# Attention beside an FFN: four fixed stages for each FFN block in an attention step

## The chip, the cores and the metric

One core of a Trainium2 chip runs the whole program. The metric is the device time of one execution in microseconds (us), the median of several runs. The core has TensorE (PE in the profile, with PEld for its weight loads), VectorE (DVE), ScalarE (ACT), GpSimd (POOL) and SyncE (SP), which here issues nearly all DMAs. Each works through its own queue in order; engines wait for each other through semaphores.

## The reference

Attention in which a query sees only the keys of its own hash bucket, and then a feed-forward network (FFN) on its result:

```python
q_bits = (np.einsum('bhsd,dk->bhsk', q, proj) > 0)      # 6 bits; k the same
mask = q_bucket[:, :, :, None] == k_bucket[:, :, None, :]
scores = np.where(mask, scale * q @ k.T, -1e9)
attn = softmax(scores)                                   # over the keys
x = (attn @ v) as [batch * seq, heads * head_dim]
h = x @ w_in
out = (h * np.clip(h + 3.0, 0.0, 6.0) / 6.0) @ w_out
```

There are 4 batches, 8 heads, 768 positions, head size 64, so 32 heads in all; x is 3072 x 512, w_in 512 x 2048, w_out 2048 x 512. All is float32. The kernel keeps that precision with products of split numbers: each operand is a rounded part (high) plus the rest (low), and high x high, high x low and low x high are summed.

## The kernel before

**Attention** goes by steps. A step handles 128 queries of one head against its 768 keys, so a head is six steps and there are NS = 192. In step k the loop does, for different rows g of the pipeline:

- `scores(k + 3)`, inside `lead` (L909): four PE matmuls into the tile s. Outside the beginning there is a single such tile (`pair`, L102, tag "s", one buffer); the hash matmuls z of the next head use the same one.
- `lowest(k + 2)` (L355): DVE reads s, writes p and its row minimum m, which frees s.
- `exponential(k + 1)` (L366): ACT, in place on p.
- `flip(k + 1)` and `move(k)` (L390, L398): from step GT on, p is turned without PE. DVE transposes 32 x 32 blocks into f, SP writes f to DRAM (fd), and four DMAs bring it back turned, into one of two tiles (`spare` for even rows, `px` for odd ones).
- `split_p` (L415): ACT casts the turned row into the high part ph, and DVE (first half of the keys) or POOL (second half) subtracts to the low part pl. Before GT the row is turned by PE transposes (pt) instead. The subtractions are collected in `lows` and issued by `split_lows` (L444).
- `value_half` and `values` (L452): at every second step, twelve PE matmuls, ph and pl of two rows times the split values vv, into acc. `output` (L470) copies acc to y on ACT, SP stores it to the DRAM tile xs, and `add` (L465) lets a POOL DMA add the other half to it.

`lead` also prepares the next head, by t = (k + 3) mod 6: at t = 0 `split_qk` (L268; ACT copy qq, three SP DMAs, POOL subtractions kk and qq), at t = 2 `split_v` (POOL) and the loads, at t = 4 `scale_q` (L261). `hash_qk` and `bits` follow at t = 2 as well.

**The FFN** goes by chunks of 256 positions, twelve in all, and by 16 blocks `fc` in each chunk. A block is `gemm1` (L562, twelve matmuls into h), `gate` (L585: ACT relu into g, DVE product with h, ACT cast into gb's first half gh, POOL or, in the last batch, DVE subtraction into gb's second half gl), and `gemm2` (L597, six wide matmuls into po), which is issued one block later. g and gb have one buffer each in this part of the program. The three chunks of batch 0 run by themselves early on. The other nine come from the generator `ffn` (L817): whatever calls `next(fill)` gets its next piece. Between chunks a list `side` holds the work that loads, normalises and splits the next chunk's inputs.

**Order.** PE, DVE, ACT and POOL stand in the order of the code (`manual_schedule`); the DMAs on SP are put in order by a scheduler when the program is built. GF = 2 * 48 + FS and GT = GF + FT set where the loop changes: `next(fill)` is first called at step GF - 2 = 102, and from step GT - 1 = 105 each step is a call of `beside_ffn` (L971). This function calls `next(fill)` twice: after `split_p` (gemm1 of a block), and after the hash (gemm2 of the block before, then the gate). What is left of the FFN when attention has ended runs alone.

Of the kernel before, what the change touches and what calls it, by code (L numbers as in the profile page):

```python
# [10 lines left out]
F32 = mybir.dt.float32  # L11
# [16 lines left out]

LA = 3
FB = 4  # L30
FS = 8
FT = 2
LT = 2
WL = 30
# [9 lines left out]
def lsh_attention_moe(  # L44
# [31 lines left out]
    def dma(out: bass.AP, in_: bass.AP):  # L76
        nonlocal last
        last = nc.sync.dma_start(out=out, in_=in_)

    ob_turn = 0  # L80
    spare = []

# [172 lines left out]
    def spans(i: int):  # L255


        n = 4 if i <= 2 else 2 if i > GF // KT + 1 else 1
        return [slice(x * S // n, (x + 1) * S // n) for x in range(n)]

    def scale_q(i: int):  # L261

        for c in spans(i):
            nc.gpsimd.tensor_scalar_mul(raws[i][:D, c], raws[i][:D, c], -SCALE)

    copied = None

# [176 lines left out]
    def split_lows():  # L444
        for f in lows:
            f()
        lows.clear()
# [135 lines left out]
        return x[:, 0], x[:, 1]  # L583

    def gate(n: str, fc: int, hp, copy, engine, between=lambda: None):  # L585
        g = sp.tile([P, TC], F32, name=f"g{n}_{fc}", tag="g", bufs=1)
        gh, gl = gate_tiles(f"{n}_{fc}")
        nc.scalar.activation(g[:], hp[:], AF.Relu, bias=three[:], scale=1.0)  # L588
        nc.vector.scalar_tensor_tensor(  # L589
            out=g[:], in0=g[:], scalar=6.0, in1=hp[:], op0=ALU.min, op1=ALU.mult  # L590
        )
        between()
        copy(gh, g[:])  # L593
        engine.tensor_sub(gl, g[:], gh.bitcast(F32))  # L594
        return gh, gl

    def gemm2(fc: int, po, gh, gl):  # L597
        wo = wt[2 * fc + 1]
# [27 lines left out]
    def beside():  # L626
        if side:
            side.pop(0)()
# [105 lines left out]
    def first_ffn(resume):  # L734
        nonlocal ffn_on
        ffn_on = True
        normalise("late0", lt(0), late["rb"][0], "pt")
        split_x(x0[0][cc3], lt(0), nc.vector)
        room12(0)
        for c in range(cc3):  # L740
            split_x(x0[1][c], xr0[1][:, c], (nc.vector, nc.gpsimd)[c % 2])
        normalise("late1", lt(1), late["rb"][1], "pt")
        yield

        room12(1)
# [12 lines left out]
        def finish(fc: int, t: int, gg):  # L758
            gemm2(fc, pos[t], *gg)
            return (lambda: store(0, t, pos[t])) if fc + 1 == NFC else None  # L760


        begun = WA
        stage = {WA - 1: 2}
        for n, (fc, t) in enumerate(order):
            if n == 1:
                pos[2] = [bank([P, DM], f"pt0_{u}", "pt")[:] for u in range(2)]
            hp = gemm1(f"0_{t}", fc, x0[t], "pu")
            new = None
            if begun < NW and n and n % 4 != 3 and n >= ready.get(begun, 0):  # L770
                new = begun
                begun += 1
            at = dict(stage)

            for x in [x for x in at if at[x] == 5]:
                cv(x)

            def between():

                if new is not None:  # L780
                    cv(new)
                for x in [x for x in at if at[x] == 3]:
                    cv(x)

            gg = gate(f"0_{t}", fc, hp, nc.scalar.copy, nc.vector, between)
# [24 lines left out]
            if n >= len(order) - 3:  # L810
                resume(n - len(order) + 3)
        yield
        finish(*pend)()
        ffn_on = False
        yield

    def ffn():  # L817
        nonlocal ffn_on
# [8 lines left out]
        def begin(c: int):  # L827
# [3 lines left out]
            xr[c] = load_x(b, t, range(NCC))  # L831
            todo = scale_x(b, t, range(NCC), xr[c])
            if b < B - 1:
                side.extend([lambda: None] * 2 + todo)
                return

            side.extend([lambda: None] * (4 if t else 6) + todo[:2])
# [28 lines left out]
        for c, (b, t) in enumerate(chunks):  # L866
            while not there(c):
                if pend is not None:
                    finish()()
                yield  # L870
            n = f"{b}_{t}"
            if c not in xr:
                begin(c)
            while side:
                beside()
                yield
                yield
            if c not in xhl:
                place(c)
                for cc in range(NCC):  # L880
# [3 lines left out]
            po = None  # L884
            for fc in range(NFC):
                hp = gemm1(n, fc, xhl[c])
                yield
                end = finish() if pend is not None else lambda: None
                if po is None:
                    po = ps.tile([P, 2, 512], F32, name=f"po{n}", tag="s" if b == B - 1 and t % 2 == 0 else "po", bufs=1)  # L890
                gg = gate(n, fc, hp, copy, engine)
                end()
                pend = ((b, t), (fc, [po[:, u] for u in range(2)], *gg))
                if c + 1 < len(chunks) and c + 1 not in xr and there(c + 1):
                    if fc >= XF[chunks[c + 1][0] == B - 1]:
                        begin(c + 1)
                if fc + 1 == NFC and c + 1 in xr and c + 1 not in xhl and not side:
                    place(c + 1)
                    for cc in range(NCC):
                        split(c + 1, cc)  # L900
                else:
                    beside()
                yield
                beside()
            del xhl[c]
        finish()()

# [1 line left out]
    def lead(j: int):  # L909
# [3 lines left out]
        alone = j < GF + LA  # L913
        if t == 0 and n < NJ:
            split_qk(n, nc.scalar.copy if ffn_on else nc.gpsimd.tensor_copy)
        if t in (1, 4):
            add()
        if t == 2:
            if i:
# [41 lines left out]
    with tc.manual_schedule(engines={ET.PE, ET.DVE, ET.Activation, ET.Pool}):  # L961
# [6 lines left out]
            ahead(0, x)  # L968
        for _ in range(2):
            cv(0)  # L970
        def beside_ffn(k: int):  # L971

            for c in range(2):
                if k < GT:
                    transp(k, c)
            whole = False
            for _ in range(1 if k < GT else 2):
                u = vnext // 2
                if u < NS // 2 and (k < GT or k % 2 == 0 and k >= 2 * u + 2 + (LT if 2 * u >= GT else 0)):
                    whole = value_half()  # L980
            if k + 1 < NS:
                exponential(k + 1)
            late = k if k < GT else k - LT
            if GT <= late < NS or k < GT:
                for c in range(2):
                    split_p(late, c, False)
            next(fill, None)
            if whole:
                output(vnext // 2 - 1)
            if k == NS + LT - 1:  # L990
# [12 lines left out]
            if k + LA < NS:  # L1003
                lead(k + LA)
            else:
                add()

        for k in range(NS + LT):
            if k >= GT - 1:
                beside_ffn(k)  # L1010
                continue
# [59 lines left out]
            if k + 1 == GB:  # L1071
# [3 lines left out]
                    whole = value_half()  # L1075
                output(vnext // 2 - 1)
                next(first)
        while vnext < NS:
            if value_half():
                output(vnext // 2 - 1)  # L1080
        add()
        for _ in fill:
            pass
# [47 lines left out]
```

## Time and profile before

| | us |
|---|---|
| median of 3 runs | 1090.09 (1090.05 to 1092.1) |
| the profiled execution | 1093.36 |
| its span in the trace | 1091.3 |

Busy time in that span: PE 994.0 us (91%), PE weight loads 894.3, DVE 707.4, ACT 623.6, POOL 567.9. A busy PE is not a PE at its peak, since the profile models the ends of matmuls and a matmul at half clock is busy twice as long. So shares of the whole say little here. The profile is read by stages: attention alone and with the first FFN chunks (to about 406 us), attention beside the FFN (to about 894 us), and the FFN alone. The starts of L360 (`lowest`, once a step) mark the steps: row 105 at 406.29 us, row 112 at 437.40, row 191 at 893.68. The granted clock of PE is 1.0 at full speed and 0.5 when it is halved.

### The profile page before, as it was taken

To read this page: it belongs to the slowest core of one execution; us is meant where nothing else is said; L and a number is where in the kernel's file an instruction comes from. 1 tells how busy PE (TensorE), PEld (TensorE's weight loads), DVE (VectorE), ACT (ScalarE), POOL (GpSimd) and SP (SyncE) were. 2 spreads that over 40 slices of the span, in tenths; PEclk is the share of its full clock that TensorE was granted. 3 is DMA by queue.
4 is the path that set the end of the run, shared out by engine and by line. 5 is a ranking of instruction groups with operands and counts; after the bars stand their busy time and mean duration, and the time that the engine had idled before them with its cause. 6 is when DMAs were issued, how large, how long until landed. Compare 5 with 4: busy or idle time off the path is not lost.

```text
span 1091.3 us, 19386 instructions
## 1 busy us (share of the span) xinstructions
PE 994.0 (91%) x6330; PEld 894.3 (82%) x6330; DVE 707.4 (65%) x1350; ACT 623.6 (57%) x1407; POOL 567.9 (52%) x662
## 2 busy tenths in 40 slices
PE   8999999999999996888888878878877999999998
PEld 7999888888899995778777768767776978899897
DVE  6999988897699996566556655656655662233332
ACT  5888865555788884455454545454445554333332
POOL 6777625565377765566556645664666453301000
PEclk8999999999999997999899999998989999999999
DMA  3566585000355556675666666675657653001000
GB/s 108 152 150 163 150 305 205 1 1 6 106 120 119 120 132 187 196 212 174 198 199 171 186 187 196 182 209 169 197 158 223 179 167 91 20 20 40 1 20 20
DMA packets 109340, 148.37 MB, mean 136 GB/s; under 512 B 12804, under 2 KB 78724, under 8 KB 109240
## 3 DMA queue, kind: packets, MB, share of 16 engines
q1 hardware_dynamic: 104760, 141.64, 42.8%
q0 software_dynamic: 4480, 5.51, 4.3%
q8 instruction: 50, 0.82, 0.3%
q14 instruction: 50, 0.41, 0.1%
HBM read 75.76 MB, written 51.90 MB: 117 GB/s over the span
## 4 chain that ended last, share of the span: by engine, by line
PE 56%; DVE 12%; DMA 9%; issue 7%; POOL 7%; ACT 6%; SPq 2%; DVEq 0%; POOLq 0%; ACTq 0%
PE pt L382 5%; PE h L569 5%; PE acc L460 5%; PE h L570 5%; PE h L568 5%; PE po L601 5%; PE po L603 5%; PE po L602 4%; PE acc L461 4%; PE s L351 4%; DMA spare<-fd 4%; PE s L353 4%; DVE pl L440 3%; DVE p L360 2%; POOL qq L298 2%
## 5 line engine op out<-in xcount | busy, mean ns | idle before, releaser
L360 DVE TENSOR_SCALAR_CACHE_REDUCE p<-s 128x768 f32<-128x768 f32 x192 | 183.5, 956 | 26.9 <-PE pt L382 13.8
L372 ACT ACTIVATE p<-p,m 128x768 f32<-128x768 f32 x192 | 179.8, 936 | 18.3 <-DVE p L360 17.7
L593 ACT CAST gb<-g 128x256 fp32r<-128x256 f32 x137 | 55.7, 407 | 213.5 <-DVE g L589 136.2
L393 DVE STREAM_TRANSPOSE f<-p 128x768 f32<-128x768 f32 x86 | 84.0, 977 | 126.3 <-ACT p L372 85.0
L588 ACT ACTIVATE g<-h,three 128x256 f32<-128x256 f32 x192 | 91.0, 474 | 128.3 <-PE h L570 112.1
L594 POOL TENSOR_TENSOR gb<-g,gb 128x256 fp32r<-128x256 f32 x89 | 65.5, 736 | 172.0 <-ACT gb L593 170.1
L460 PE MATMUL acc<-ph,vv 128*128 128x256 f32 x564 | 151.0, 299 | 2.5 <-DVE pl L440 2.4
L589 DVE SCALAR_TENSOR_TENSOR g<-g,h 128x256 f32<-128x256 f32 x192 | 80.0, 417 | 108.6 <-ACT g L588 108.0
L568 PE MATMUL h<-xh,w 128*128 128x256 f32 x512 | 146.4, 286 | 0.7 <-ACT xh L559 0.7
L461 PE MATMUL acc<-pl,vv 128*128 128x256 f32 x564 | 142.9, 286 | 4.3 <-DVE pl L440 4.3
L569 PE MATMUL h<-xl,w 128*128 128x256 f32 x512 | 145.6, 284 | 0.2 <-DVE xl L560 0.2
L570 PE MATMUL h<-xh,w 128*128 128x256 f32 x512 | 144.7, 283 | 0.0
L351 PE MATMUL s<-kk,qq 76*128 76x384 f32 x384 | 108.1, 363 | 27.3 <-DVE p L360 25.3
L461 PEld LDWEIGHTS acc<-pl,vv 128*128 128x128 f32 x564 | 109.1, 193 | 5.3 <-DVE pl L440 5.2
L460 PEld LDWEIGHTS acc<-ph,vv 128*128 128x128 f32 x564 | 108.9, 193 | 5.4 <-PE pt L382 2.0
L439 ACT CAST ph<-pt 128x384 fp32r<-128x384 f32 x204 | 91.4, 473 | 26.7 <-PE pt L382 15.8
L440 DVE TENSOR_TENSOR pl<-pt,ph 128x384 fp32r<-128x384 f32 x204 | 104.0, 550 | 2.5 <-ACT ph L439 1.9
L353 PE MATMUL s<-kk,qq 128*128 128x384 f32 x384 | 103.3, 351 | 0.0
L351 PEld LDWEIGHTS s<-kk,qq 76*128 76x128 f32 x384 | 65.2, 197 | 46.4 <-DVE p L360 28.0
L601 PE MATMUL po<-w,gb 128*128 128x512 f32 x242 | 100.3, 414 | 3.0 <-ACT ob L617 2.0
L569 PEld LDWEIGHTS h<-xl,w 128*128 128x128 f32 x512 | 97.9, 191 | 3.1 <-DVE xl L560 0.6
L568 PEld LDWEIGHTS h<-xh,w 128*128 128x128 f32 x512 | 97.8, 191 | 2.6 <-ACT xh L559 1.0
(163 smaller groups left out, 2552.4 us busy)
## 6 DMA issues: line engine op xcount, KB each, us to landing
fd<-f SPq DMA_DIRECT2D x86, 384.0 KB, 3.5
spare<-fd SPq DMA_DIRECT2D x172, 96.0 KB, 2.6
px<-fd SPq DMA_DIRECT2D x172, 96.0 KB, 2.7
raw<-in_qkT SPq DMA_DIRECT2D x32, 384.0 KB, 3.3
kk<-qq SPq DMA_DIRECT2D x62, 192.0 KB, 3.2
wr<-in_w_in SPq DMA_DIRECT2D x16, 512.0 KB, 10.8
wr<-in_w_out SPq DMA_DIRECT2D x16, 512.0 KB, 3.9
vr<-in_v SPq DMA_DIRECT2D x32, 192.0 KB, 2.6
```

The costliest lines, as they stand in the source:

```text
L351: nc.tensor.matmul(s[:, c, :HW], lhsT=q1[:KM, us], rhs=half(k1[:KM], c), start=True, stop=False)
L353: nc.tensor.matmul(s[:, c, :HW], lhsT=q2[:, us], rhs=half(k2, c), start=False, stop=True)
L360: nc.vector.tensor_scalar(out=pr_[:], in0=s[:, :, :HW], scalar1=CAP, scalar2=None, op0=ALU.min, op1=ALU.min, accum_out=m[:],)
L372: nc.scalar.activation(pr_[:], pr_[:], AF.Exp, bias=m[:], scale=-1.0, accum_out=sms[b][:, t, h : h + 1])
L439: nc.scalar.copy(hi, pt)
L440: lows.append(lambda: engine.tensor_sub(lo, pt, hi.bitcast(F32)))
L460: nc.tensor.matmul(acc[:], lhsT=vv[:, kt], rhs=hi[:, x], start=(kt == 0), stop=False)
L461: nc.tensor.matmul(acc[:], lhsT=vv[:, kt], rhs=lo[:, x], start=False, stop=(kt == KT - 1))
L568: nc.tensor.matmul(hp[:], lhsT=wi[:, 0, wc], rhs=xh, start=(cc == 0), stop=False)
L569: nc.tensor.matmul(hp[:], lhsT=wi[:, 0, wc], rhs=xl, start=False, stop=False)
L570: nc.tensor.matmul(hp[:], lhsT=wi[:, 1, wc], rhs=xh, start=False, stop=(cc == NCC - 1))
L601: nc.tensor.matmul(po[u], lhsT=gh[:, us], rhs=wo[:, 0], start=(fc == 0), stop=False)
```

## The change

Each block of the FFN beside attention is cut into four stages, A to D, and `beside_ffn` has one place for each. `go("A")` runs the generator only if that is the stage it stands at.

- A, after the exponential: the split of the gate (gh on ACT, gl on POOL) of the block begun in the step before. `gate` now returns a function that does it.
- B, after the casts `split_p`: gemm1. (The pieces before the first block run here too, one a step.)
- C, after minimum, outputs and hash: gemm2 of the block before, and relu and product of this block.
- D, at the end of the step: the work of `side`.

Other edits in the same function: `split_lows` (pl on DVE and POOL) stands behind stage C and `lead` instead of ahead of them; `output` runs in the step after its values; `add` runs at k mod 6 = 2 and 4, behind D, instead of in `lead`. `scale_q` runs on ACT once `paced` is set, and `spans` no longer cuts the later heads in two. FS goes from 8 to 10, so the first call of the generator is at step 104 and `beside_ffn` starts at step 107. The loop runs two steps longer, without attention rows. When it ends, blocks go on unstaged as before.

```diff
-FS = 8
+FS = 10
@@ spans, scale_q
-        n = 4 if i <= 2 else 2 if i > GF // KT + 1 else 1
+        n = 4 if i <= 2 else 1
...
+            if paced:
+                nc.scalar.mul(raws[i][:D, c], raws[i][:D, c], -SCALE)
+            else:
+                nc.gpsimd.tensor_scalar_mul(raws[i][:D, c], raws[i][:D, c], -SCALE)
@@ gate
         between()
-        copy(gh, g[:])
-        engine.tensor_sub(gl, g[:], gh.bitcast(F32))
-        return gh, gl
+        def split():
+            gh, gl = gate_tiles(f"{n}_{fc}")
+            copy(gh, g[:])
+            engine.tensor_sub(gl, g[:], gh.bitcast(F32))
+            return gh, gl
+        return split
@@ ffn
                 hp = gemm1(n, fc, xhl[c])
+                stage = "C"
                 yield
                 end = finish() if pend is not None else lambda: None
...
+                parted = paced
+                split_g = gate(n, fc, hp, copy, engine)
+                if not parted:
+                    gg = split_g()
                 end()
...
+                if parted:
+                    stage = "D"
+                    yield
+                    for _ in range(-(-len(side) // (NFC - fc))):
+                        beside()
                 if fc + 1 == NFC and c + 1 in xr and c + 1 not in xhl and not side:
                     place(c + 1)
                     for cc in range(NCC):
                         split(c + 1, cc)
-                else:
+                elif not parted:
                     beside()
+                if parted:
+                    stage = "A"
+                    yield
+                    gg = split_g()
+                pend = ((b, t), (fc, [po[:, u] for u in range(2)], *gg))
+                stage = "B"
                 yield
-                beside()
+                if not parted:
+                    beside()
@@ lead
-        if t in (1, 4):
+        if t in (1, 4) and not paced:
             add()
@@ beside_ffn
                 if u < NS // 2 and (k < GT or k % 2 == 0 and k >= 2 * u + 2 + (LT if 2 * u >= GT else 0)):
-                    whole = value_half()
+                    if value_half():
+                        through.append(vnext // 2 - 1)
             if k + 1 < NS:
                 exponential(k + 1)
+            go("A")
             late = k if k < GT else k - LT
             if GT <= late < NS or k < GT:
                 for c in range(2):
                     split_p(late, c, False)
-            next(fill, None)
-            if whole:
-                output(vnext // 2 - 1)
+            go("B")
...
             if k + 2 < NS:
                 lowest(k + 2)
+            paced = True
+            while through and (through[0] < vnext // 2 - 1 or k % 2 or k < GT):
+                output(through.pop(0))
+            if k + LA < NS and (k + LA) % KT == 2 and (k + LA) // KT + 1 < NJ:
+                hash_qk((k + LA) // KT + 1)
+                bits((k + LA) // KT + 1)
+            go("C")
+            if k + LA < NS:
+                lead(k + LA)
             split_lows()
             if GT <= k < NS:
                 move(k)
-            if k + LA < NS and (k + LA) % KT == 2 and (k + LA) // KT + 1 < NJ:
-                hash_qk((k + LA) // KT + 1)
-                bits((k + LA) // KT + 1)
-            next(fill, None)
-            if k + LA < NS:
-                lead(k + LA)
-            else:
+            go("D")
+            if k % KT in (2, 4):
                 add()
-        for k in range(NS + LT):
+        for k in range(NS + LT + 2):
```

Where this puts instructions is shown at one place of the program, steps 147 and 148, where head 26 is split. In the names, kk_26 and qq_26 are that head's low parts, pl72 and ph72 the parts of rows 144 (from `spare`) and 145 (from `px`), with _0 or _1 for the half of the keys, and gb1_2_4 is the gate of batch 1, chunk 2, block 4.

POOL before:

```order
L264 TENSOR_SCALAR raw26_7959<-raw26_7959 64x384 x2
L440 TENSOR_TENSOR pl72_1_8100<-spare_5537,ph72_1_8099 128x3x128
L594 TENSOR_TENSOR gb1_2_4_8139<-g1_2_4_8138,gb1_2_4_8139 128x256
L440 TENSOR_TENSOR pl72_1_8100<-px_5704,ph72_1_8099 128x3x128
L594 TENSOR_TENSOR gb1_2_5_8185<-g1_2_5_8184,gb1_2_5_8185 128x256
L296 TENSOR_TENSOR kk_26_8190<-raw26_7959,qq_26_8191 64x384 x2
L298 TENSOR_TENSOR qq_26_8191<-raw26_7959,qq_26_8191 64x384 x2
L440 TENSOR_TENSOR pl73_1_8223<-spare_5537,ph73_1_8222 128x3x128
```

POOL of the changed kernel at the same place (its lines are numbered a little higher):

```order
L602 TENSOR_TENSOR gb1_2_1_8019<-g1_2_1_7990,gb1_2_1_8019 128x256
L445 TENSOR_TENSOR pl72_1_8026<-spare_5610,ph72_1_8025 128x3x128
L602 TENSOR_TENSOR gb1_2_2_8069<-g1_2_2_8054,gb1_2_2_8069 128x256
L301 TENSOR_TENSOR kk_26_8107<-raw26_7862,qq_26_8108 64x768
L303 TENSOR_TENSOR qq_26_8108<-raw26_7862,qq_26_8108 64x768
L445 TENSOR_TENSOR pl72_1_8026<-px_5780,ph72_1_8025 128x3x128
L602 TENSOR_TENSOR gb1_2_3_8140<-g1_2_3_8104,gb1_2_3_8140 128x256
L445 TENSOR_TENSOR pl73_1_8147<-spare_5610,ph73_1_8146 128x3x128
```

The scale (raw26) is gone from POOL. The low part of row 145, pl72_1 from px, stood ahead of kk_26 and qq_26 and now stands behind them. On PE the matmuls acc72, which read pl72_1, stand in both kernels right behind the scores of row 150, the last work of step 147.

ACT before, from the exponential of step 147 on:

```order
L372 ACTIVATE p148_8124,sms3_7905<-p148_8124,m148_8123 128x768
L439 CAST ph72_0_8096<-px_5704 128x3x128
L439 CAST ph72_1_8099<-px_5704 128x3x128
L588 ACTIVATE g1_2_5_8184<-h1_2_5_8152,three_68 128x256
L593 CAST gb1_2_5_8185<-g1_2_5_8184 128x256
L290 CAST qq_26_8191<-raw26_7959 128x768
L372 ACTIVATE p149_8170,sms3_7905<-p149_8170,m149_8169 128x768
```

ACT of the changed kernel:

```order
L377 ACTIVATE p148_8046,sms3_7811<-p148_8046,m148_8045 128x768
L601 CAST gb1_2_2_8069<-g1_2_2_8054 128x256
L444 CAST ph72_0_8022<-px_5780 128x3x128
L444 CAST ph72_1_8025<-px_5780 128x3x128
L490 COPY y23_2_8094<-acc71_8005 64x256
L593 ACTIVATE g1_2_3_8104<-h1_2_3_8074,three_68 128x256
L295 CAST qq_26_8108<-raw26_7862 128x768
L377 ACTIVATE p149_8092,sms3_7811<-p149_8092,m149_8091 128x768
L601 CAST gb1_2_3_8140<-g1_2_3_8104 128x256
```

The cast gb of a block stood between its relu (L588, now L593) and the next exponential; now it stands behind that exponential.

SP before, which the scheduler orders:

```order
L78 DMA fd148_8167<-f148_8165 128x768
L78 DMA px_5704<-fd147_8121 32x4x192 x4
L78 DMA kk_26_8190<-qq_26_8191 64x768
L78 DMA qq_26_8191<-qq_26_8191 64x768
L78 DMA kk_26_8190<-qq_26_8191 64x768
L78 DMA fd149_8242<-f149_8240 128x768
```

SP of the changed kernel:

```order
L78 DMA fd148_8089<-f148_8087 128x768
L78 DMA xs2_127<-y23_2_8094 64x256
L78 DMA kk_26_8107<-qq_26_8108 64x768
L78 DMA qq_26_8108<-qq_26_8108 64x768
L78 DMA kk_26_8107<-qq_26_8108 64x768
L78 DMA fd149_8164<-f149_8162 128x768
L78 DMA raw27_8238<-in_qkT 128x768
L78 DMA px_5780<-fd147_8043 32x4x192 x4
```

The four transfers that bring row 147 back into px, which must wait until both halves of row 145 have been split, now stand behind the write of row 149.

More of the change, by code (lines that the diff above doesn't have):

```diff
@@ L78, in dma @@
         last = nc.sync.dma_start(out=out, in_=in_)
+    paced = False
+    stage = "B"
     ob_turn = 0
@@ L263, in scale_q @@
         for c in spans(i):
-            nc.gpsimd.tensor_scalar_mul(raws[i][:D, c], raws[i][:D, c], -SCALE)
+            if paced:
+                nc.scalar.mul(raws[i][:D, c], raws[i][:D, c], -SCALE)
+            else:
+                nc.gpsimd.tensor_scalar_mul(raws[i][:D, c], raws[i][:D, c], -SCALE)
     copied = None
@@ L586, in gate @@
         g = sp.tile([P, TC], F32, name=f"g{n}_{fc}", tag="g", bufs=1)
-        gh, gl = gate_tiles(f"{n}_{fc}")
         nc.scalar.activation(g[:], hp[:], AF.Relu, bias=three[:], scale=1.0)
@@ L783, in between @@
                     cv(x)
-            gg = gate(f"0_{t}", fc, hp, nc.scalar.copy, nc.vector, between)
+            gg = gate(f"0_{t}", fc, hp, nc.scalar.copy, nc.vector, between)()
             for x in [x for x in at if at[x] == 2]:
@@ L817, in ffn @@
     def ffn():
-        nonlocal ffn_on
+        nonlocal ffn_on, stage
         chunks = [(b, t) for b in range(1, B) for t in range(NTC)]
@@ L833, in begin @@
             if b < B - 1:
-                side.extend([lambda: None] * 2 + todo)
+                side.extend([lambda: None] * (0 if paced else 2) + todo)
                 return
@@ L869, in ffn @@
                     finish()()
+                stage = "B"
                 yield
@@ L875, in ffn @@
                 beside()
+                stage = "B"
                 yield
-                yield
+                if not paced:
+                    yield
             if c not in xhl:
@@ L890, in ffn @@
                     po = ps.tile([P, 2, 512], F32, name=f"po{n}", tag="s" if b == B - 1 and t % 2 == 0 else "po", bufs=1)
-                gg = gate(n, fc, hp, copy, engine)
+                parted = paced
+                split_g = gate(n, fc, hp, copy, engine)
+                if not parted:
+                    gg = split_g()
                 end()
-                pend = ((b, t), (fc, [po[:, u] for u in range(2)], *gg))
                 if c + 1 < len(chunks) and c + 1 not in xr and there(c + 1):
@@ L900, in ffn @@
                         split(c + 1, cc)
-                else:
+                elif not parted:
                     beside()
+                if parted:
+                    stage = "A"
+                    yield
+                    gg = split_g()
+                pend = ((b, t), (fc, [po[:, u] for u in range(2)], *gg))
+                stage = "B"
                 yield
-                beside()
+                if not parted:
+                    beside()
             del xhl[c]
@@ L970, in lsh_attention_moe, with go @@
             cv(0)
+        def go(part: str):
+            if stage == part:
+                next(fill, None)
+        through = []
         def beside_ffn(k: int):
+            nonlocal paced, stage
             for c in range(2):
@@ L975, in beside_ffn @@
                     transp(k, c)
-            whole = False
             for _ in range(1 if k < GT else 2):
@@ L986, in beside_ffn @@
                     split_p(late, c, False)
-            next(fill, None)
-            if whole:
-                output(vnext // 2 - 1)
-            if k == NS + LT - 1:
+            go("B")
+            if k == NS + LT:
                 homes.clear()
@@ L1077, in lsh_attention_moe @@
                 next(first)
-        while vnext < NS:
-            if value_half():
-                output(vnext // 2 - 1)
+        paced = False
+        assert vnext == NS and not through
         add()
```

## The prediction

> **What bounds the kernel now.** First the stages, as busy time of each engine in four stretches (columns: length, then PE, weight load, DVE, ACT and POOL with counts, granted clock, DMA share, GB/s): attention up to step 105, the passage to the form beside the FFN, attention and FFN together, FFN alone.
>
> ```profile
> 0.00:406.00 406.00, 394.89 (x2686) 363.07 (x2687) 352.34 (x713) 298.91 (x656) 254.59 (x292) 0.99 0.45 123
> 406.00:437.40 31.40, 21.09 (x109) 18.18 (x108) 20.57 (x39) 14.87 (x34) 18.02 (x22) 0.74 0.62 174
> 437.40:893.70 456.30, 388.58 (x2322) 343.30 (x2322) 270.49 (x449) 236.47 (x550) 266.95 (x307) 0.94 0.65 190
> 893.70:1091.30 197.60, 189.48 (x1219) 169.75 (x1218) 64.00 (x152) 73.37 (x168) 28.29 (x43) 1.00 0.11 33
> ```
>
> The first and the last stage are PE-bound and hardly touched. The third is the one that matters: 79 steps (scores 113 to 191, one FFN block each) in 456.3 us, 5.78 a step, with 67.7 us of PE idle and a mean clock of 0.94. What PE needs at the full clock is read from its timeline, where one kind of work starts and the next follows:
>
> ```profile
> 511.54 0.28 PE L460 MATMUL acc<-ph,vv 128*128 128x256 f32 x1
> ...
> 512.95 0.28 PE L568 MATMUL h<-xh,w 128*128 128x256 f32 x1
> ...
> 514.36 0.39 PE L601 MATMUL po<-w,gb 128*128 128x512 f32 x1
> ...
> 515.75 0.54 PE L351 MATMUL s<-kk,qq 76*128 76x384 f32 x2
> ...
> 516.48 0.28 PE L568 MATMUL h<-xh,w 128*128 128x256 f32 x1
> ```
>
> Values 1.41 us (every second step), first product h 1.41, second product po 1.39, scores 0.73. So a step with values is 4.94, one without 3.53, and a head of six with its six hash matmuls (z, as wide as scores, about 0.18 each) 26.5, or 4.42 a step. The stage's own busy time says a little more: a clock of 0.94 is 12% of 456.3, 55 us, at half speed, which cost 27 us; 388.6 - 27 = 361.6 over 79 steps is **4.57 a step** (normalising transposes and the ends of matmuls are in it). I use that. The stage thus has 95 us above its PE work.
>
> Who holds PE up? The next rows are waits from 450 to 895 us (engine and line, what it waited for, total, times, longest).
>
> ```profile
> PE z L305 <- DVE p L360: 34.8, 11, 7.1
> PE s L351 <- DVE p L360: 17.1, 16, 2.3
> PE rt L526 <- POOL spare L516: 9.7, 8, 2.2
> ...
> DVE f L393 <- ACT p L372: 82.8, 50, 2.4
> DVE f L393 <- DMA fd<-f: 25.1, 10, 5.7
> ...
> ACT gb L593 <- DVE g L589: 100.3, 50, 4.3
> ACT gb L593 <- PE po L603: 64.2, 20, 7.9
> ...
> POOL gb L594 <- ACT gb L593: 145.8, 63, 7.7
> ```
>
> PE waits for the minimum (p, L360) that frees the scores' bank; DVE waits for the exponential; ACT waits, in front of the exponential, for DVE's gate product. That is a ring, and a quiet step shows it whole (DVE's rows, then ACT's):
>
> ```profile
> 641.67 0.98 DVE L393 STREAM_TRANSPOSE f<-p 128x768 f32<-128x768 f32 x1 [1.46 <-ACT p L372]
> 642.77 0.96 DVE L360 TENSOR_SCALAR_CACHE_REDUCE p<-s 128x768 f32<-128x768 f32 x1
> 643.66 0.08 DVE L360 DVE_READ_ACCUMULATOR p<-s 128x1 f32 x1
> 643.66 0.55 DVE L440 TENSOR_TENSOR pl<-px,ph 128x384 fp32r<-128x384 f32 x1
> 644.13 0.41 DVE L589 SCALAR_TENSOR_TENSOR g<-g,h 128x256 f32<-128x256 f32 x1
> ...
> 642.36 0.47 ACT L588 ACTIVATE g<-h,three 128x256 f32<-128x256 f32 x1
> 644.63 0.41 ACT L593 CAST gb<-g 128x256 fp32r<-128x256 f32 x1 [1.80 <-DVE g L589]
> 644.94 0.93 ACT L372 ACTIVATE p<-p,m 128x768 f32<-128x768 f32 x1
> ```
>
> Transpose f, minimum, low part pl, gate product, rounded gate gb, exponential, next transpose: from 641.67 to about 646.0, 4.33 us with nothing to spare. Whatever else enters it (query copy, bits, a stretched pl) lengthens the step.
>
> **The change part by part.** All durations are of this execution (span 1091.3; the median of the runs shown is 1.2 below it, so I subtract the difference from the median).
>
> *Gate split a stage later (A), low parts after the gate (C).* gb now stands behind the exponential in ACT's order and pl behind the gate product in DVE's. No instruction is added. The ring shrinks to minimum, exponential, transpose: 0.96 + 0.93 + 0.98 plus gaps, some 3.1 us, under PE's 4.57. What is next late? From the end of h: relu 0.47, exponential 1.1, gb 0.41, gl 0.74, with gaps 3.0; PE meanwhile has po, scores and the next h, 3.53, or 4.94 with values. It fits, by 0.5 at the least. The 64.2 us in which gb waited for po to free its single buffer go too, since that po is finished 1.4 us after h.
>
> *Query scale on ACT, one span per head.* These groups (total us, mean ns) carry the prices of what leaves POOL and of what stays; the 64x768 rows are from the stages before, where heads are split in one piece:
>
> ```profile
> L264 POOL TENSOR_SCALAR raw<-raw 64x384 f32<-64x384 f32 x22 | 28.5, 1443 | 0.0
> L440 DVE TENSOR_TENSOR pl<-spare,ph 128x384 fp32r<-128x384 f32 x39 | 43.3, 1110 | 0.0
> L440 DVE TENSOR_TENSOR pl<-px,ph 128x384 fp32r<-128x384 f32 x39 | 22.0, 565 | 0.0
> L276 ACT ACTIVATE qq<-raw 64x768 fp32r<-64x768 f32 x1 | 0.8, 844 | 2.0 <-DMA raw<-in_qkT 2.0
> L290 ACT CAST qq<-raw 128x768 fp32r<-128x768 f32 x11 | 9.1, 829 | 0.0
> L296 POOL TENSOR_TENSOR kk<-raw,qq 64x768 fp32r<-64x768 f32 x6 | 11.0, 1836 | 0.5
> L298 POOL TENSOR_TENSOR qq<-raw,qq 64x768 fp32r<-64x768 f32 x6 | 11.1, 1842 | 0.5
> L440 POOL TENSOR_TENSOR pl<-px,ph 128x384 fp32r<-128x384 f32 x39 | 41.7, 1068 | 29.0 <-ACT ph L439 19.0 <-DMA spare<-fd 10.0
> L594 POOL TENSOR_TENSOR gb<-g,gb 128x256 fp32r<-128x256 f32 x77 | 56.7, 736 | 147.7 <-ACT gb L593 145.8 <-PE s L353 1.8
> ```
>
> POOL loses 2 x 1.44 = 2.9 us a head; ACT gains one 0.84, the same operation and width, in a step where ACT has the time. DVE's pl beside it, 1.11 against 0.57 for the other buffer, should come near 0.57.
>
> *What is next late: POOL's low part behind the next head's split.* In the step with k mod 6 = 3 (I call it the splitting step) POOL's queue is now gl, kk, qq, then pl of that step's row; before, pl stood ahead of kk and qq. The values of the very next step read that pl. With the splitting step's h starting at 0: h ends 1.41, relu 2.0, ACT's copy (0.83) 2.8, kk 2.9 to 4.7, qq 6.6, pl 7.7. PE is through with po and scores at 3.5, the values' first half at 4.2, and stands before the first low part at about 4.3. That is a **new wait of 3.4 us a head**. Behind it on PE stand the next h and po, and relu and everything after waits for that h. It comes in the splitting steps 117 to 177, 11 of them (the last two heads split nothing).
>
> Does that gap also lower the clock? Two gaps of before, each window with the one behind it:
>
> ```profile
> 516.80:520.20 3.40, 1.24 (x11) 1.03 (x9) 0.95 (x1) 2.46 (x6) 3.32 (x5) 1.00 0.90 263
> 520.20:523.60 3.40, 2.14 (x7) 2.06 (x8) 1.46 (x4) 0.00 (x0) 0.54 (x1) 0.51 0.95 271
> 482.70:486.10 3.40, 1.85 (x15) 1.65 (x13) 1.34 (x3) 2.63 (x6) 3.32 (x5) 1.00 0.78 248
> 486.10:489.50 3.40, 2.25 (x11) 2.07 (x12) 2.48 (x4) 0.00 (x0) 1.16 (x2) 1.00 0.90 256
> ```
>
> 2.2 us idle in a window of 3.4 is followed by 3.4 us at half clock, 1.55 is not. A gap of 3.4 puts 2 us into one window in some four of five positions; half a window of work, 1.7, is then lost at most. I take 1.4 a gap; bounds 0 and 3.4 (two windows). The Trainium skill, "TensorE: Matmul & The Clock Gate", Part 1, asks for a whole idle window (about 3.4 us) before the clock falls; the trace disagrees, at 2.2 us. By that rule the gap would cost no clock, and the sum would be 15 us less.
>
> *Outputs a step later, adds at k mod 6 = 2 and 4.* The same instructions. The accumulator is held one step longer, which is hidden as four banks turn over three tiles in two steps. Bounds: 0 to one wait of 0.4 a head, the copy's length; I take 0.
>
> *FFN begun later, fewer FFN steps.* Two more steps run in the old form, with PE transposes. Six minima of that form stand between 394.6 and 406.3:
>
> ```profile
> L360 DVE TENSOR_SCALAR_CACHE_REDUCE p<-s x6: 956/958/958, 394.6 to 406.3; 128x768 f32<-128x768 f32 x6
> ```
>
> 2.34 a step, so +4.7. The FFN's first h now stands before scores 115, not 113: 77 steps with a block instead of 79, and 62 blocks behind the last values instead of 60, so 2 x 2.80 = +5.6 at the end. The passage keeps its 31.4 (bounds 26 and 36: about one step).
>
> *Hand-over of chunks.* Four inputs are split and four results stored: ACT's four casts and two stores now stand before an exponential. I take 8 us in all; bounds 0 and 16 (the rt row above is 9.7 today).
>
> **Sum.** 406.0 + 4.7 + 31.4 + [77 x 4.57 = 352, 11 x (3.4 + 1.4) = 53, 8] 413 + 203.2 = 1058.3, against 1091.3: -33. On the median: **1057**. With the bounds of clock (-15, +22), passage (5) and hand-over (8) added up one way, 1029 to 1092.
>
> **Rivals.**
> (1) *The clock holds* in the new gap: 11 x 1.4 less, 1042. The row at 516.80 speaks against it, the one at 482.70, with 1.55 idle and no fall, a little for it. The Trainium skill, "TensorE: Matmul & The Clock Gate", Part 1, has the rule that would bring this.
> (2) *No new wait*: POOL reaches kk early enough and all steps run at PE's pace: 413 becomes 360, 1004. Against it: ACT's copy follows relu in its queue, and relu needs h; the 7.7 above has no slack in it.
> (3) *The transfer ring*: the next f needs the buffer that the write to fd still reads.
>
> ```profile
> fd<-f SPq DMA_DIRECT2D x77, 384.0 KB, 3.5
> ```
>
> 0.98 + 3.5 = 4.5 already, and DVE waited 25.1 us for it. A faster pace lifts the DMA share from 0.65 towards 0.8. If the landing grows by 1 us, the step is 5.5: 77 x 5.5 = 424, with some 1.5 left of each gap 440, 1084. For it: fd is near the limit. Against: steps of 4.33 ran, and on SP the write of row 149 stands ahead of the transfers that wait for the late pl, so the new wait does not hold fd up.
> (4) *Slower*: the splitting step's 3.7 us of kk and qq stay as a backlog on POOL; behind them come gl, pl, the adds, then the next step's split of values and pl, and the values two steps on wait a second time, with a second fall of the clock. By the timeline above that later pl is done some 1.5 us before it is needed; it decides once shared work stretches POOL by more than that. Second waits of 3.4 + 1.7 add 56: 1113. From 3.0 a head on it eats the whole gain.
> (5) *It does not do what it says*: a block misses its stage and is left for the end. The order shows one h and one po in each of the 77 steps, so this is nearly excluded; price 2.80 a block, so 12 blocks to come back to 1090.
>
> **How the numbers follow.** Forecast 0.57; clock holds 0.08; no wait 0.07; transfer ring 0.14; slower 0.12; blocks missed 0.02. The range from 1025 to 1092 takes in the forecast's bounds, (1), (3) and (5) and leaves out (2) and (4), 0.19. About 0.2%, 2 us, is what a measurement of this kernel can tell from no change: faster 0.85, the same 0.03 (the upper end of the forecast and of (3), and (5)), slower 0.12.
>
> **What would show it.** Right: ACT's gb hardly waits for g; z L305 hardly waits for the minimum; PE's longest waits are now for pl from POOL, some 3.4 us, 11 times, with half-clock windows after most; steps between them near 4.6. The clock rival shows as 1.00 there, the transfer ring as f waiting for fd in most steps, the slower case as two waits for pl a head. Wrong would be a third stage above 450 us, or a wait for pl that is missing.

## The result, and the profile after

The changed kernel takes 1074.85 us (median, 1071.87 to 1075.61) against 1091.09 for the kernel before: a ratio of 0.9845, with a 95% interval of 0.9821 to 0.9869. So it is faster by 16 us. The forecast was 1057: the direction is right and the time lies in the range, but the gain is a little under half of the 33 that were forecast. The profiled execution took 1075.23, its span is 1073.5.

The stages again, cut where the steps of the changed kernel change (row 114 starts at 441.21, row 191 at 870.08); columns as before:

```profile
0.00:406.00 406.00, 393.66 (x2698) 361.67 (x2699) 354.76 (x716) 300.05 (x659) 255.14 (x291) 1.00 0.45 123
406.00:441.20 35.20, 23.81 (x128) 20.13 (x126) 23.67 (x43) 17.66 (x40) 20.15 (x21) 0.74 0.63 179
441.20:870.10 428.90, 378.00 (x2257) 343.61 (x2257) 246.46 (x437) 241.39 (x547) 223.53 (x252) 0.92 0.67 195
870.10:1073.50 203.40, 196.88 (x1265) 175.65 (x1263) 65.56 (x156) 75.69 (x173) 32.01 (x48) 1.00 0.11 34
```

Three of the four came out as summed: the FFN stage begins at 441.2 (forecast 442.1) and the end takes 203.4 (forecast 203.2). The third is 428.9 where 413 were forecast, so the error is there. PE is idle for 50.9 of it, and its clock is 0.92, lower than the 0.94 of before.

The waits in that stage, PE's from 441.2 to 870.1, then DVE's, ACT's and POOL's from 450 to 870:

```profile
PE acc L466 <- POOL pl L445: 35.6, 11, 3.6
PE z L310 <- DVE p L365: 8.9, 5, 3.6
PE s L356 <- DVE p L365: 3.5, 6, 1.1
...
DVE f L398 <- DMA fd<-f: 33.3, 25, 2.4
...
DVE f L398 <- ACT p L377: 9.5, 6, 2.9
...
ACT gb L601 <- DVE g L594: 14.3, 10, 2.0
ACT gb L601 <- PE po L613: 9.4, 9, 3.8
...
POOL gb L602 <- ACT gb L601: 105.9, 54, 6.7
```

The old ring is open: DVE waits 9.5 us for the exponential where it waited 82.8, ACT's cast 14.3 for the gate product where it waited 100.3, and PE's waits for the minimum are down from 52 us to 12. The new wait is the one forecast: eleven times, 3.2 us on average, for POOL's low part. One of them, in the splitting step of head 25, on POOL and then on PE:

```profile
604.58 1.01 POOL L602 TENSOR_TENSOR gb<-g,gb 128x256 fp32r<-128x256 f32 x1
606.96 1.84 POOL L301 TENSOR_TENSOR kk<-raw,qq 64x768 fp32r<-64x768 f32 x1 [1.38 <-ACT qq L295]
608.86 1.80 POOL L303 TENSOR_TENSOR qq<-raw,qq 64x768 fp32r<-64x768 f32 x1
610.74 1.00 POOL L445 TENSOR_TENSOR pl<-px,ph 128x384 fp32r<-128x384 f32 x1
...
608.32 0.28 PE L465 MATMUL acc<-ph,vv 128*128 128x256 f32 x1
611.79 0.58 PE L466 MATMUL acc<-pl,vv 128*128 128x256 f32 x1 [3.19 <-POOL pl L445]
```

PE stands from 608.6 to 611.8, until pl, behind kk and qq, is through. What follows is where the forecast was too low. Windows of 3.4 us, laid on the edges at which the granted clock changes; first the gap above and what comes after it, then the gap of head 30:

```profile
607.30:610.70 3.40, 1.30 (x11) 1.06 (x9) 2.29 (x4) 1.25 (x4) 3.31 (x2) 1.00 0.89 251
610.70:614.10 3.40, 2.31 (x11) 2.31 (x12) 0.00 (x0) 0.51 (x1) 2.41 (x4) 0.51 0.78 242
614.10:617.50 3.40, 3.40 (x13) 3.01 (x13) 0.89 (x2) 1.39 (x3) 1.40 (x2) 0.50 0.45 99
617.50:620.90 3.40, 2.89 (x20) 2.58 (x19) 1.84 (x3) 2.01 (x6) 2.24 (x4) 0.99 0.42 116
...
778.00:781.40 3.40, 0.35 (x3) 0.14 (x2) 1.95 (x3) 0.51 (x1) 3.26 (x4) 1.00 0.82 231
781.40:784.80 3.40, 3.35 (x15) 3.35 (x16) 0.00 (x0) 0.51 (x1) 2.02 (x3) 0.50 0.95 219
784.80:788.20 3.40, 3.40 (x23) 3.09 (x22) 1.49 (x4) 2.79 (x7) 0.41 (x2) 1.00 0.39 87
```

In the first the gap lies across two windows: 2.1 us idle come ahead of the fall of the clock, and with the 1.1 us that are left of the gap in the low window it stays down for a second one. In the other nearly the whole gap lies in one window, and the clock is low for one. Eight falls lasted two windows, with 0.67 us or more idle in the first low one, and four lasted one, with at most 0.04. With 2.3 us left over from the passage they add up to 70.6 us at half clock between rows 114 and 191 (the granted-clock record); in the kernel before it was 52.1, from 437.4 to 893.7. Each of the eleven waits for pl brings a fall, seven of them for two windows and four for one, together 61.4 us. The twelfth fall belongs to another wait, of the hash for the minimum (3.6 us, up to 448.4), behind a transpose that had waited 2.8 us for fd.

### The profile page after: what moved, and what is told of

It reads as the page before. It is cut to its first block, busy times and chain, and to the rows that moved or that the text cites. A ratio compares the mean times of both kernels' runs of the same rounds, so it can differ in the third digit from the quotient of the medians.

```text
span 1073.5 us, 19263 instructions
## 1 busy us (share of the span) xinstructions
PE 992.4 (92%) x6342; PEld 901.1 (84%) x6342; DVE 690.5 (64%) x1350; ACT 634.8 (59%) x1418; POOL 530.8 (49%) x608
## 4 chain that ended last, share of the span: by engine, by line
PE 39%; DMA 5%; POOL 4%; issue 3%; DVE 3%; ACT 2%; SPq 2%; DVEq 0%; POOLq 0%; ACTq 0%
PE h L574 5%; PE h L575 5%; PE h L573 5%; PE po L611 5%; PE po L613 5%; PE po L612 5%; PE acc L466 3%; DMA fd<-f 2%; PE acc L465 2%; POOL qq L303 2%; SPq L78 2%; PE s L356 1%; PE s L358 1%; DVE f L398 1%; POOL pl L445 1%
## 5 line engine op out<-in xcount | busy, mean ns | idle before, releaser
L365 DVE TENSOR_SCALAR_CACHE_REDUCE p<-s 128x768 f32<-128x768 f32 x192 | 183.4, 956 | 26.3 <-PE pt L387 12.4
L593 ACT ACTIVATE g<-h,three 128x256 f32<-128x256 f32 x192 | 91.2, 475 | 177.3 <-PE h L575 154.5
L466 PE MATMUL acc<-pl,vv 128*128 128x256 f32 x564 | 149.7, 296 | 40.9 <-POOL pl L445 36.7
L465 PE MATMUL acc<-ph,vv 128*128 128x256 f32 x564 | 154.6, 303 | 3.3 <-DVE pl L445 3.3
L573 PE MATMUL h<-xh,w 128*128 128x256 f32 x512 | 151.2, 295 | 0.7 <-ACT xh L564 0.7
L575 PE MATMUL h<-xh,w 128*128 128x256 f32 x512 | 149.6, 292 | 0.0
L574 PE MATMUL h<-xl,w 128*128 128x256 f32 x512 | 149.4, 292 | 0.0
L356 PE MATMUL s<-kk,qq 76*128 76x384 f32 x384 | 103.0, 349 | 11.4 <-DVE p L365 8.0
L444 ACT CAST ph<-pt 128x384 fp32r<-128x384 f32 x208 | 93.1, 474 | 25.2 <-PE pt L387 14.3
L573 PEld LDWEIGHTS h<-xh,w 128*128 128x128 f32 x512 | 102.9, 201 | 2.7 <-ACT xh L564 1.0
L574 PEld LDWEIGHTS h<-xl,w 128*128 128x128 f32 x512 | 102.9, 201 | 1.7 <-DVE xl L565 0.2
L575 PEld LDWEIGHTS h<-xh,w 128*128 128x128 f32 x512 | 102.8, 201 | 0.0
L358 PE MATMUL s<-kk,qq 128*128 128x384 f32 x384 | 101.1, 345 | 0.0
L611 PE MATMUL po<-w,gb 128*128 128x512 f32 x242 | 100.0, 413 | 0.9 <-ACT gb L601 0.8
L613 PE MATMUL po<-w,gb 128*128 128x512 f32 x242 | 98.7, 408 | 1.2 <-POOL gb L602 0.9
```

The source lines that it names most:

```text
L356: nc.tensor.matmul(s[:, c, :HW], lhsT=q1[:KM, us], rhs=half(k1[:KM], c), start=True, stop=False)
L358: nc.tensor.matmul(s[:, c, :HW], lhsT=q2[:, us], rhs=half(k2, c), start=False, stop=True)
L365: nc.vector.tensor_scalar(out=pr_[:], in0=s[:, :, :HW], scalar1=CAP, scalar2=None, op0=ALU.min, op1=ALU.min, accum_out=m[:],)
L465: nc.tensor.matmul(acc[:], lhsT=vv[:, kt], rhs=hi[:, x], start=(kt == 0), stop=False)
L466: nc.tensor.matmul(acc[:], lhsT=vv[:, kt], rhs=lo[:, x], start=False, stop=(kt == KT - 1))
L573: nc.tensor.matmul(hp[:], lhsT=wi[:, 0, wc], rhs=xh, start=(cc == 0), stop=False)
```

## The experiments

Two theories of the missing 16 us were set against each other. A: the wait for pl is as forecast, and the clock that it lowers costs more than the 1.4 us a gap of the sum. B: something else sets the pace now (transfers, hand-over), and PE's gaps only show it.

**Low parts first.** One line moved:

```diff
             go("C")
+            split_lows()
             if k + LA < NS:
                 lead(k + LA)
-            split_lows()
```

> The changed kernel with one line moved: the low parts pl are issued ahead of the next head's preparation (lead), still behind stage C. So POOL has gl, pl, kk, qq in the splitting step and the next gl behind qq. Theory A (the new wait for pl and the clock that it lowers are what the change lost: 35.6 us of waiting in 11 places, 68 us at half clock beside the FFN, which cost 34): the waits for pl go, a wait of about 1 us a head for gl at the second product comes, most half-clock windows go: 1018 to 1030 us, against 1075. Rival B (the stage is held by the transfers f to fd and the hand-over of chunks, and PE merely waits elsewhere): 1060 to 1075.

Measured: 1046.37 us, ratio to the kernel before 0.960 (0.9557 to 0.9644). That is 28 us less than the changed kernel, half-way between the two expectations. The stage takes 402.4, its half-clock time is 25.5. PE's longest waits (450 to 870 us):

```profile
PE z L310 <- DVE p L365: 26.0, 11, 5.8
PE po L613 <- POOL gb L602: 7.1, 10, 0.9
```

The wait for pl is gone and the one for gl is there, smaller than expected. But the hash now waits 26.0 us for the minimum. So A holds for the gap, but PE's idle time in the stage falls only from 50.9 to 40.8: other waits have taken the place of most of the 35.6 us. Of the hash's eleven waits, four (13.9 of the 26.0 us, the two long ones of 5.9 and 5.0 among them) stand behind a transpose that had waited for the write to fd, as B said. Ahead of six the transpose waited for ACT, ahead of one it followed other DVE work. The longest, on DVE and then on PE:

```profile
538.58 0.98 DVE L398 STREAM_TRANSPOSE f<-p 128x768 f32<-128x768 f32 x1 [5.66 <-DMA fd<-f]
539.68 0.96 DVE L365 TENSOR_SCALAR_CACHE_REDUCE p<-s 128x768 f32<-128x768 f32 x1
...
540.70 0.66 PE L310 MATMUL z<-qq,pjl 128*108 128x384 f32 x1 [5.85 <-DVE p L365]
```

**The gap filled.** PE gets 28 more matmuls at the place where it waits. pjl's first 64 columns are zero, so they add zero to the accumulator:

```diff
             nc.tensor.matmul(acc[:], lhsT=vv[:, kt], rhs=hi[:, x], start=(kt == 0), stop=False)
+            if fillers and c == 1 and x == 0:
+                for _ in range(NFILL):
+                    nc.tensor.matmul(acc[:D], lhsT=pjl[:, :D], rhs=hi[:, x], start=False, stop=False)
...
+            fillers = k > GT + LT and k % KT == 4 and k < NS - KT - LA
```

> The changed kernel with 28 more matmuls in each of 12 splitting heads, in the place where PE waits for pl: they add zero times ph to the same accumulator, 28 x 0.118 = 3.3 us, about the wait itself. The wait stays, PE is busy in it. Theory A: the clock stays at 1.0 through the gap, the 68 us at half clock nearly go, and the time falls by 25 to 34 us, to 1041 to 1052. Rival B (the lowered clock hides in slack; the other engines set the pace): 1070 to 1080, whatever the clock does. Rival C (the falls come from other gaps): the half-clock windows stay.

Measured: 1058.91 us, ratio 0.9722 (0.9678 to 0.9766). PE does 336 matmuls more and the kernel is 16 us faster than the changed one. The stage:

```profile
446.60:853.40 406.80, 389.39 (x2563) 356.65 (x2562) 248.87 (x436) 241.34 (x547) 224.90 (x252) 0.99 0.70 205
```

The half-clock time falls from 70.6 to 10.2 us and the stage from 428.9 to 406.8, by 22.1. The stage begins 5.4 us later, though: one of the 12 places lies ahead of it, where the clock is still at 0.50. This settles that the lowered clock costs time by itself, with the wait still there. The whole gain of 16 us is less than the 25 to 34 that A expected, and the time lies between the ranges of A and B: of the 30 us that 60 us at half clock lose, 22 come back in the stage.

**The gap half filled**, NFILL = 16 in place of 28.

> The changed kernel with 16 of the zero matmuls in each of the 12 gaps instead of 28: 1.9 us of work, so that 1.2 to 1.7 us of each gap stay idle. Theory A (a threshold: the clock falls after a window of 3.4 us with some 1.9 us or more idle, and stays low for another window unless that one is nearly full): these gaps lower the clock no more, and the time is that of the filled gap, 1056 to 1063. Rival B (the clock follows the share of idle time): about half the gain of the filled gap, 1064 to 1070, and half the half-clock time.

Measured: 1060.28 us, ratio 0.9733 (0.9705 to 0.9762), as with the gap filled. PE still waits:

```profile
PE acc L471 <- POOL pl L445: 15.3, 10, 1.8
```

That is 1.5 us a gap, yet the half-clock time is 13.7 us. So here the clock follows a threshold and not the idle share, as A said: gaps of 1.5 us lowered it hardly more often than filled ones.

**The scale back on POOL** in the changed kernel, one span (`if paced:` becomes `if False:` in scale_q).

> The changed kernel with the query scale back on POOL, in one piece of about 2.2 us a head, in the step with k mod 6 = 1, ahead of that step's pl. Theory A: POOL has room for it there (pl is done at about 4.0 us of the step and needed at 4.4), DVE's pl meets it sometimes: 1073 to 1082. Rival B (moving the scale was a main part of the gain): 1085 or more.

Measured: 1079.78 us, ratio 0.9904 (0.9874 to 0.9934): 5 us more than the changed kernel, inside what A expected. DVE's pl beside it (from px) is stretched to 0.64 us on average, and POOL's scale takes 2.13.

**The scale alone on ACT**, in one span, in the kernel before:

```diff
-        n = 4 if i <= 2 else 2 if i > GF // KT + 1 else 1
+        n = 4 if i <= 2 else 1
...
+            if i > GF // KT + 1:
+                nc.scalar.mul(raws[i][:D, c], raws[i][:D, c], -SCALE)
+            else:
+                nc.gpsimd.tensor_scalar_mul(raws[i][:D, c], raws[i][:D, c], -SCALE)
```

> The kernel before with the query scale of the heads beside the FFN on ACT and one span, and nothing else. Theory A (the ring of transpose, minimum, low part, gate product, gate cast, exponential sets the steps): DVE's stretched pl comes back from 1.1 to about 0.6 us (8 x 1.8 = -14), ACT's 0.84 a head now stands in the ring (+9), the one-piece kk and qq change little: 1080 to 1090. Rival B (POOL's load was what held the kernel before): 1075 or less.

Measured: 1082.00 us, ratio 0.9921 (0.9894 to 0.9949). So this part alone, with the split in one piece that comes with it, is worth 9 us, and the ring stays: ACT's cast still waits 109.8 us for the gate product (450 to 890 us). A's range holds it; its account of DVE's pl does not quite, since that came down from 1.11 to 0.92 us and not to 0.6:

```profile
L443 DVE TENSOR_TENSOR pl<-spare,ph 128x384 fp32r<-128x384 f32 x39 | 35.9, 919 | 0.0
```

**The gate in one piece**, in the kernel with the low parts first:

```diff
                 parted = paced
                 split_g = gate(n, fc, hp, copy, engine)
-                if not parted:
-                    gg = split_g()
+                gg = split_g()
...
                     stage = "A"
                     yield
-                    gg = split_g()
```

> The kernel with the low parts first, but the split of the gate back in stage C, so that ACT's cast gb stands ahead of the exponential again, behind the gate product and behind the second product that frees gb. Theory A (the deferred split is a main part of the gain): gb waits for po again, exponential, transpose and minimum come 1 to 2 us later, the hash waits more, the clock falls more often: 1058 to 1078 against 1046. Rival B (moving pl behind the gate product alone had opened the ring): 1045 to 1052.

Measured: 1118.63 us, ratio 1.0275 (1.0238 to 1.0311): 72 us more than with the low parts first alone, and slower than the kernel before. ACT's waits (450 to 840 us):

```profile
ACT gb L601 <- PE po L613: 66.9, 35, 6.3
ACT gb L601 <- DVE g L594: 47.7, 29, 4.6
```

These are the two waits of the kernel before, back in front of the exponential. The direction is A's, the size far above it. Part of the 72 us is not the ring's: the low parts stand behind gl in this order, so they now wait with it, and PE waits for pl 37 times, 25.5 us.

**The second subtraction a step later**, in the kernel with the low parts first: qq's is put into a list, which the next step empties behind its own split_lows.

```diff
+        def second():
             for c in spans(i + 1):
                 nc.gpsimd.tensor_sub(q2[D:, c], raw[:D, c], q1[:D, c].bitcast(F32))
+        if paced:
+            later.append(second)
+        else:
+            second()
...
             split_lows()
+            if later:
+                later.pop()()
             if k + LA < NS:
                 lead(k + LA)
```

> The kernel with the low parts first, and POOL's second subtraction of the head's split (qq, 1.85 us) issued one step later, behind that step's pl. Theory A (what is left there is the gate's low part gl behind kk and qq: relu waits for it to free g, and the exponential, transpose, minimum and hash behind it come late): the waits of relu for gl (20.6 us) and part of the hash's 26 us go, 1030 to 1041 against 1046. Rival B (the hash waits because the transfers f to fd are late): 1044 to 1050.

Measured: 1053.76 us (1046.39 to 1056.6), ratio 0.9668 (0.9623 to 0.9712): no gain over 1046.37, rather a loss. Relu's waits for gl fall from 20.6 us to 3.3, as A had it, but the hash waits 35.1 us instead of 26.0. The edit brought a cost of its own, which neither theory had. POOL's moved subtraction now runs beside the low part that DVE computes in the hash's step, and that low part takes 1.6 to 1.8 us in ten of these steps in place of 0.55. The group with the low parts first and then in this run (450 to 840 us):

```profile
L445 DVE TENSOR_TENSOR pl<-spare,ph 128x384 fp32r<-128x384 f32 x38 | 21.0, 552 | 0.0
L452 DVE TENSOR_TENSOR pl<-spare,ph 128x384 fp32r<-128x384 f32 x37 | 31.4, 848 | 0.0
```

The transpose and the minimum stand behind it. So the run does not decide what gl costs: the gain that A forecast did not come, but a new delay stood against it. That the transfers hold the hash up, as B has it, is seen in four of the eleven waits above and fits the 37 us in which DVE's transpose waits for fd in this run (38.8 with the low parts first), but no run changes the transfers alone.

**Begun as before**, FS at 8, in the changed kernel and with the low parts first.

> The changed kernel with FS at 8 again, so that FFN begins two steps earlier. Theory A: two more steps beside the FFN at 5.57 us, two fewer old steps at 2.34 and two fewer blocks at the end at 2.80: +0.9, so 1072 to 1080 with the spread of the runs. Rival B (the later beginning keeps the passage short or long): outside that by more than 4.

> Low parts first, and FS at 8. Theory A (a step beside the FFN costs 5.23 us in the kernel with the low parts first, so two more of them for two old steps at 2.34 and two blocks at 2.80 are even): 1042 to 1050, as with FS at 10. Rival B (the earlier beginning itself is worth the 6 us that it seemed to give the changed kernel): 1036 to 1041.

Measured: 1068.59 us (ratio 0.9829, 0.9787 to 0.9871) and 1047.20 (0.959, 0.9553 to 0.9626). With the low parts first the beginning makes no difference, as A said. In the changed kernel it came out 6 us lower, outside A's range, though not by the 4 that B asked for. Its half-clock time is 49.5 us (rows 112 to 191) instead of 70.6, with waits for pl of much the same length (29.6 us in 10 places, against 35.6 in 11). Most of its falls last one window, so what differs is probably where the gaps lie in the windows; no run shifts the gaps alone. The two intervals overlap.

**The changed kernel again.**

> The changed kernel once more, unaltered, on the chip of the run above. Theory A: 1071 to 1077, so that the 28 us between it and the low parts first are no difference of chips. Rival B (chips differ as much as these kernels do): 1060 or less, or 1085 or more.

Measured: 1073.63 us (1067.31 to 1076.21), ratio 0.982 (0.9761 to 0.9878). The 28 us between it and the low parts first are no matter of chips.

## Why the prediction was right and wrong

- *PE's pace between the gaps, 4.57 a step*: right, slightly high. 378.0 us busy less half of 70.6 is 342.7 for 77 steps, 4.45. (As in the forecast, PE is taken as busy throughout the low windows; it was idle for some 9 us of them, which would make it 4.5.)
- *The ring opens*: right. Its waits are the ones that went, and with the gate in one piece they came back, in a kernel that is 72 us slower.
- *The scale*: right in price (0.83 us on ACT). Both pl of DVE stand at 0.55 and 0.57 us after the change. It is worth 9 us in the kernel before and 5 in the changed one.
- *The new wait for pl, 3.4 us, 11 times*: right, 35.6 us in 11 places, and the place too. Taking it out gave 28 us.
- *Two old steps more, two blocks more at the end, passage, outputs later*: right to 1 us in the sum; the experiment with FS at 8 finds nothing else in them when the gap is away.
- *The clock's price of a gap*: **this is the step that failed**: "I take 1.4 a gap". The mechanism was right, the gaps did lower the clock, but the term was mis-sized. All eleven gaps brought the clock down, not four in five, and seven of the falls lasted two windows: 61.4 us at half clock, at full price 30.7, or 2.8 a gap. Filling the gaps gives 22.1 us in the stage, 2.0 a gap. The sum had 15.4, so the term was 7 to 15 us too low, of the 16. The second window, which the forecast had as a bound only, could be read from the kernel before: the fall behind the row at 516.80 went on for another window, as four of the eleven falls of that stage did.

```profile
523.60:527.00 3.40, 3.40 (x10) 2.82 (x9) 1.50 (x2) 0.72 (x3) 0.23 (x1) 0.50 0.38 103
```

- *Hand-over and the rest, 8*: too low by about 7. PE is idle for 50.9, of which 35.6 are for pl. The other 15.3 are mainly the hash and the scores behind the minimum (12.4), while DVE's transpose waits 33.3 us for fd. The rival of the transfer ring was thus not wholly wrong: with the low parts first it is behind about half of the hash's waits.
- *The stage's 16 us by busy and idle time*: half clock 35.3 us where the sum had 15.4, idle time apart from pl 15.3 for 8, the wait for pl 35.6 for 37.4, PE's work 342.7 for 351.9. That is +20, +7, -2 and -9. That the time came out within the range is thus owed in part to terms that missed in opposite directions.
- *Rivals*: that the clock holds is refuted, by the windows above. The Trainium skill, "TensorE: Matmul & The Clock Gate", Part 1, lets the clock fall after an idle window of about 3.4 us; here 2.1 us idle in a window were enough. That no new wait comes is refuted by the 35.6 us. The slower case, a second wait for pl in each head, did not come, and no blocks were left over: the end took the 203.4 us of the forecast.

## What to carry to other kernels

When a ring of waits is opened by moving work between stages, look for what the moved work now stands behind on its own engine: here one line, the low parts ahead of the next head's preparation, gives the changed kernel another 28 us (1046 us, the best version found). Price a gap on PE by its length and by the clock behind it, and look in the trace for how long the clock stayed down after earlier gaps. Where the gap itself can't be closed, cutting its idle part to about 1.5 us with harmless matmuls paid here: 1.9 us of useless work in each gap gave 14 us.

## What the runs showed of the hardware that was not expected

The granted clock falls at one share of idle time and rises again at another. In the traces it changes in steps of 3.41 us: its low stretches last 3.41 or 6.83 us, seldom more. Over the ten traces of before, after and the first eight experiments (from 430 us on, idle time of PE in windows laid on the clock's own edges), 89 falls followed windows with 1.35 us idle or more, nearly all over 1.7, and none of some 1620 windows without a fall had more than 1.84. So a gap of 3.2 to 3.6 us, as most were here, comes to that size wherever it lies, for one of two windows gets 1.6 us of it or more. But to rise again a low window had to be nearly full: the 89 that were followed by the full clock had at most 0.64 us idle, the 29 that were followed by another low one at least 0.67, but for one with 0.26. So a gap is paid for twice when 0.67 us or more of it run on into the low window. Counted as work at full speed the two limits lie closer, since a window at half clock that is busy for 2.8 us does 1.4 us of such work, while every full-speed window with less than 1.6 us of it was followed by a fall, and some with up to 2.1. Which of the two the chip counts no run shows.
